# Fused chunked scan and two feed-forward layers: the order of halves, weight sums and wide rounds around a pair of token tiles

## The chip, the core and the metric

The kernel runs as one program on one core of a Trainium2 chip. The metric is device time in microseconds (us): the median of several executions, each the time of the whole program. A profile is one further execution, recorded by the hardware profiler. Engines are named as the profile names them: PE (TensorE matmul; PEld its weight load), DVE (VectorE), ACT (ScalarE), POOL (GpSimd), SP (SyncE, which here issues nearly all DMAs).

## The reference

Shapes: batch 4, 8 heads, 768 positions, head size 32, state size 16; so 3072 tokens of 256 features. All is float32.

```python
# per chunk c: cum = cumsum(log a), state carried from chunk to chunk
M = (Cc @ Bc^T) * exp(cum_i - cum_j) * (i >= j)
y = M @ xc + (Cc @ state) * exp(cum)
state = exp(sum log a) * state + sum_j Bc_j (x) xc_j * exp(cum_last - cum_j)
# tokens x 256, d_ff 768
x = maximum(maximum(x @ w1, x @ w2), x @ w3) @ w_out
# d_ff 2048
h = x @ w_in
out = (maximum(h, 0) + alpha * minimum(h, 0)) @ w_out2
```

## The kernel before

**Numbers.** Every float32 operand of a large product is kept as two parts, high (`gh`, index 0) and low (`gl`, index 1). A product of two blocks is three matmuls (`parts`, L658): high by high, low by high, high by low. `split` makes the parts: ACT copies the high part (L142), then POOL or, where the call says so, DVE subtracts it from the source (L143). The names in the traces are those of the tiles: `up` and `at` are PSUM tiles of products, `g` the result of a nonlinearity, `e` copies in SBUF.

**Attention.** The scan goes over 24 blocks of 128 tokens (`NR`). Each block is a round, cut into steps that a list `todo` holds; the two layers take steps from it between their products, at a rate that `quota` works out. The steps of a block are: `att_a` (POOL scales b and c), `att_s` (ACT and POOL make the parts of b and c in one tile, `tok`), `att_t` (DVE transposes `tok` and SP writes it to DRAM, `sc<-ts`, L394 to L400), `att_l` (SP reads it back in another order, `v<-sc` and `st<-sc`, L428 and L430), `att_e` (ACT exponentials, POOL mask), `att_b` (PE multiplies c by b, L473; DVE multiplies by the decay, L475), `att_u` (state; it also issues the broadcast load `e<-cum_w` of the next block), `att_y` (PE makes y, L541 and L544). From round 6 on the order is that of `fine`; the list entries of a round are: (1) a and half of e; (2) y, u and s; (3) b; (4) t; (5) l; (6) the loads of b, c and x and the other half of e.

**Layers.** Tiles of 512 tokens go through layer 1 (three up products per block of 128 features, a maximum, a down product) and layer 2 (one up product, a leaky rectifier, a down product). The last two tiles are the **pair**. For them `pair1` and `pair` use a scheme with seven block products in place of eight: blocks a11 to a22 of the weights, b11 to b22 of the tokens, sums s1 to s4 of the former and t1 to t4 of the latter. One such group is a **quad**, n = 0 to 7 in layer 1 (`QUADS1`), with f, j = divmod(n, 3); j is which of w1, w2, w3. A quad's PE order is a11, s2, s1, a12, s4, s3, (a11 of the next quad, in `begin`), a22. `keep` copies a PSUM tile to SBUF on ACT (L931); PE may only go on adding to that tile after it. DVE adds the kept tiles at L983 and L1019 (j > 0) or L986 (j = 0). After j = 2 a block of features is whole: `ready` splits it and puts its down product on the list `downs`, and `go_down` issues one (six matmuls); `POPS` says in which quads.

**Weight sums.** s1 to s4 come from `quad_sums(n)` in three steps: an addition of 128x512 (L812, POOL), four additions of 128x128 (L815 to L818, DVE), a split (ACT, POOL). The first three quads' sums are made by `prepare` during the last tile before the pair; in `pair1` quad n steps through `quad_sums(n + 2)`, all three steps within that quad:

```python
            more = quad_sums(n + 2) if n else None
...
            if j == 2:
                ready(tb, f, nc.vector)
                ready(ta, f)
                ready(ta, f2)
                held.append((tb, f2))
```

The third product of the last features is done plainly (`plain1`, four of them). `rows` and `columns` then make t1 to t4 for layer 2, and `pair` begins layer 2 with three plain up products, two down products and a fourth up product.

Of the kernel before, what the change touches and what calls it, by code (L numbers as in the profile page):

```python
# [15 lines left out]
ALU = mybir.AluOpType  # L16
# [9 lines left out]
NR = BT * NB  # L26
# [10 lines left out]
HALF = NF2 // 2  # L37
# [3 lines left out]
QUADS1 = 3 * HALF1 - 1  # L41
# [47 lines left out]
def fused(ctx: ExitStack, tc: tile.TileContext, x, a, B, C, w1, w2, w3, w_out, v_in, v_out, alpha, cst, out):  # L89
# [443 lines left out]
    def att_y(r):  # L533
# [41 lines left out]
            nc.vector.tensor_tensor(xt[t][1][:, g, o], yp[g], xt[t][0][:, g, o], ALU.subtract)  # L575
        del blk[r]

    def rounds(r0):

        for r in range(r0, NR):  # L580
            if r >= FINE:
                yield from fine(r)
                continue
            if r + 2 < NR:
                yield lambda r=r: att_a(r + 2), 0
            yield lambda r=r: (att_y(r), r + 1 < NR and att_u(r + 1)), r + 1
            if r + 2 < NR:
                late = r + 2 == NDIR
                yield lambda r=r, late=late: (att_e(r + 1), late or att_s(r + 2)), 0
                yield lambda r=r, late=late: (att_b(r + 1), att_s(r + 2) if late else att_t(r + 2)), 0  # L590
                yield lambda r=r, late=late: (late and att_t(r + 2), att_l(r + 2), load(r + 3)), 0
            elif r + 1 < NR:
                yield lambda r=r: att_e(r + 1), 0
                yield lambda r=r: att_b(r + 1), 0
# [208 lines left out]
    def corner(n):  # L803
        f, j = divmod(n, 3)
        if n < QUADS1:
            return [w[:, j].rearrange("p k (h f) -> p h k f", h=2)[:, :, :, f * P:(f + 1) * P] for w in w123]
        q = PLAIN + n - QUADS1
        return [w.rearrange("p k (h f) -> p h k f", h=2)[:, :, :, q * P:(q + 1) * P] for w in vi]

    def quad_sums(n):  # L810
        v, u = (v_tile().bitcast(F32).rearrange("p (i f) -> p i f", i=4) for _ in range(2))
        nc.gpsimd.tensor_tensor(v.rearrange("p (h k) f -> p h k f", h=2), *corner(n), ALU.add)  # L812
        yield
        a11, a12, a21, a22 = (v[:, i, :] for i in range(4))
        nc.vector.tensor_tensor(u[:, 0, :], a21, a22, ALU.add)  # L815
        nc.vector.tensor_tensor(u[:, 1, :], u[:, 0, :], a11, ALU.subtract)
        nc.vector.tensor_tensor(u[:, 3, :], a12, u[:, 1, :], ALU.subtract)
        nc.vector.tensor_tensor(u[:, 2, :], a11, a21, ALU.subtract)  # L818
        yield
        split(*[w[:, n % NSUM] for w in sums_0], u)  # L820
        yield
# [34 lines left out]
    def columns():  # L856
        p = acc[1, PAIR[1]]
        t1 = step(tall[0], p[0], ALU.subtract)
        t2 = step(tall[1], t1, ALU.subtract)

        def more():
            t4 = step(p[1], t2, ALU.subtract)
            split(*sum_b[0], t1, nc.vector)
            split(*sum_b[1], t2)
            later.append(lambda: split(*sum_b[3], t4))

        later.append(more)
# [3 lines left out]
    def prepare():  # L871
        nc.vector.tensor_scalar(rest, alph, -1.0, 1.0, ALU.mult, ALU.add)
        for n in range(NSUM):
            yield from quad_sums(n)
        while todo:
            yield
        yield from sums_of_x()
# [23 lines left out]
    def block(p, a, b, n, first):  # L901
        w, r = stationary(a, n), moving(b, n)
        parts(p, [w[0]], [w[1]], [r], first, True)
# [25 lines left out]
    def keep(p):  # L929
        e = em.tile([P, 512], F32, tag="e", name="e")  # L930
        nc.scalar.activation(e, p, AF.Copy)  # L931
        return e
# [10 lines left out]
    def pair1():  # L943
# [16 lines left out]
        def go_down():  # L960
            if carry:
                carry.pop(0)()
            elif downs:
                t, f, h = downs.pop(0)
                down((1, t), f, 0, 512, h)
                if f == NF1 - 1:
                    leave1((1, t))

        def ready(t, f, engine=nc.gpsimd):
            h_, l_ = place1()  # L970
            split(h_, l_, g[t, f], engine)
            downs.append((t, f, (h_, l_)))
# [21 lines left out]

        a, b = begin(0)
        later.pop()()
        for n in range(QUADS1):
            f, j = divmod(n, 3)
            f2 = HALF1 + f
            if carry:  # L1000
                go_down()
            more = quad_sums(n + 2) if n else None
            block(a, "s2", "t2", n, False)
            u2 = keep(a)
            c = ptile(ps_up, "up")
            block(c, "s1", "t1", n, True)
            p5 = keep(c)
            block(b, "a12", "b21", n, False)
            top(tb, f, j, b)
            more and next(more, None)  # L1010
            if carry or 0 in POPS.get(n, ()):
                go_down()
            block(c, "s4", "b22", n, False)
            both(c, u2, ta, f, j)
            while held:
                ready(*held.pop(0))
            block(a, "s3", "t3", n, False)
            if j:
                nc.vector.tensor_tensor(p5, a, p5, ALU.add)  # L1019
                top(ta, f, j, c)  # L1020
                top(ta, f2, j, p5)
            else:
                both(a, p5, ta, f2, j)
            if n + 1 < QUADS1:
                after = begin(n + 1)
            more and next(more, None)
            if 1 in POPS.get(n, ()):
                go_down()
            block(a, "a22", "t4", n, False)
            top(tb, f2, j, a)  # L1030
            more and next(more, None)
            if j == 2:
                ready(tb, f, nc.vector)
                ready(ta, f)
                ready(ta, f2)
                held.append((tb, f2))
            if n + 1 < QUADS1:
                a, b = after
        f, f2 = HALF1 - 1, NF1 - 1
        more = quad_sums(QUADS1 + 2)  # L1040

        def plain1(t, f):
            p = up_mm([w[:, 2, :, f * P:(f + 1) * P] for w in w123], xt[t], 0, 512)
            top(t, f, 2, p)
            ready(t, f, nc.vector if f == f2 else nc.gpsimd)

        for _ in range(3):
            next(more, None)
        for t, f, n in ((ta, f, 0), (ta, f2, 1), (tb, f, 1), (tb, f2, 1)):
            plain1(t, f)  # L1050
            for _ in range(n):
                go_down()
        rows()
        while downs:
            go_down()
        columns()

    def pair():
        ta, tb = PAIR
# [24 lines left out]
        def plain(t, f):  # L1084
            p = up_mm([w[:, :, f * P:(f + 1) * P] for w in vi], yt[t], 0, 512)
            return t, f, rectify(p, f)

        u = plain(ta, 0)
        u2 = plain(ta, HALF)
        ready(*u)  # L1090
        u = plain(tb, 0)
        ready(*u2)
        later.pop()()
        go_down()
        ready(*u)
        go_down()
        held = plain(tb, HALF)
        more = prepare_a(1)
        for q in range(PLAIN, HALF - 1):
            f, f2 = q, HALF + q  # L1100
# [205 lines left out]
```

## Time and profile before

| | us |
|---|---|
| median of 3 runs | 568.26 |
| lowest and highest | 565.99, 568.77 |
| the profiled execution, its own time | 564.66 |
| its span, first to last instruction | 562.9 |
| mean granted TensorE clock | 0.984 |

| engine | busy us | share of span |
|---|---|---|
| PE | 535.5 | 95% |
| DVE | 369.9 | 66% |
| ACT | 269.3 | 48% |
| POOL | 269.8 | 48% |

The granted clock is a share of full speed (1.0 is 2.4 GHz, 0.5 is 1.2 GHz); a busy PE at 0.5 does half the work. The attention ends at about 374 us of the span, layer 1 of the pair runs from about 393 to 471, layer 2 of the pair after it.

### The profile page before, as it was taken

How to read it: one execution, taken by the hardware profiler on the slowest of the kernel's cores; microseconds unless marked ns; L12 is line 12 of the kernel's file. 1: busy time of each engine (PE TensorE's matmuls, PEld its weight loads, DVE VectorE, ACT ScalarE, POOL GpSimd, SP SyncE). 2: the span in 40 equal slices, each digit the busy share in tenths (PEclk: the TensorE clock that was granted, in tenths of full speed). 3: DMA queues.
4: the chain of work that ended last, by engine and by line, in shares of the span. 5: the costliest groups of instructions: out<-in, count | busy, mean ns of one | idle time of the engine just before them, and what ended most of it. 6: DMA issues, size and time to landing. Idle time of an engine off the chain costs nothing.

```text
span 562.9 us, 9656 instructions
## 1 busy us (share of the span) xinstructions
PE 535.5 (95%) x3378; PEld 427.6 (76%) x3379; DVE 369.9 (66%) x657; ACT 269.3 (48%) x641; POOL 269.8 (48%) x287
## 2 busy tenths in 40 slices
PE   8889999999999989999999999989979878999997
PEld 4778888887888878878887887758757756778886
DVE  5886885989964357664456677768465655676453
ACT  6667775565444324443244234413443525666651
POOL 2143443335563326554236455747364651785651
PEclk9998999999999999999999999979989999999999
DMA  8877886786645665655744566400200000000024
GB/s 147 222 159 169 204 164 174 190 196 182 143 114 106 127 137 118 132 119 123 139 116 99 109 127 146 95 0 1 38 0 1 0 0 2 1 2 0 1 37 113
DMA packets 209344, 55.60 MB, mean 99 GB/s; under 512 B 159632, under 2 KB 201168, under 8 KB 209296
## 3 DMA queue, kind: packets, MB, share of 16 engines
q1 hardware_dynamic: 206928, 54.46, 43.8%
q10 hardware_dynamic: 2368, 0.52, 0.4%
q8 instruction: 27, 0.44, 0.4%
q14 instruction: 21, 0.17, 0.1%
HBM read 44.35 MB, written 10.62 MB: 98 GB/s over the span
## 4 chain that ended last, share of the span: by engine, by line
PE 64%; DVE 11%; ACT 7%; issue 7%; DMA 5%; POOL 3%; SPq 2%; ACTq 0%; DVEq 0%; POOLq 0%
PE up L658 31%; PE acc L658 21%; PE at L658 6%; DMA e<-cum_d 2%; POOL gl L143 1%; ACT gh L142 1%; DMA sc<-ts 1%; PE at L473 1%; PE at L544 1%; ACT e L456 1%; DVE v L184 1%; DVE g L684 1%; DMA b<-in_B_dram 1%; DMA xm<-in_x_dram 1%; SPq L400 1%
## 5 line engine op out<-in xcount | busy, mean ns | idle before, releaser
L143 POOL TENSOR_TENSOR gl<-g,gh 128x512 fp32r<-128x512 f32 (+1 forms) x102 | 128.8, 1263 | 174.1 <-ACT gh L142 165.6
L142 ACT ACTIVATE gh<-g 128x512 fp32r<-128x512 f32 (+1 forms) x107 | 64.7, 607 | 168.4 <-DVE g L697 104.7
L658 PE MATMUL up<-xt,w 128*128 128x512 f32 (+1 forms) x621 | 135.6, 362 | 0.7 <-ACT xt L574 0.6
L658 PEld LDWEIGHTS up<-xt,w 128*128 128x128 f32 x621 | 105.3, 193 | 20.6 <-issue 2.4
L658 PE MATMUL up<-yt,vi 128*128 128x512 f32 x459 | 117.7, 393 | 0.0
L658 PEld LDWEIGHTS up<-yt,vi 128*128 128x128 f32 x459 | 86.9, 190 | 18.4
L658 PE MATMUL acc<-gh,vo 128*128 128x512 f32 x268 | 84.9, 398 | 0.0
L696 DVE TENSOR_SCALAR g<-up,alph 128x512 f32<-128x512 f32 x64 | 47.7, 745 | 31.1 <-PE up L658 28.2
L684 DVE TENSOR_TENSOR g<-up,g 128x512 f32<-128x512 f32 (+1 forms) x60 | 34.7, 578 | 39.7 <-PE up L658 37.7
L658 PEld LDWEIGHTS acc<-gh,vo 128*128 128x128 f32 x268 | 49.6, 190 | 10.9 <-issue 0.6
L658 PE MATMUL acc<-gl,vo 128*128 128x512 f32 x134 | 53.0, 395 | 0.2
L697 DVE SCALAR_TENSOR_TENSOR g<-up,g 128x512 f32<-128x512 f32 x64 | 44.2, 691 | 2.2
L456 ACT ACTIVATE e<-e,ncum 128x128 f32<-128x128 f32 x120 | 38.0, 388 | 0.0
L658 PE MATMUL acc<-gh,wo 128*128 128x512 f32 (+1 forms) x136 | 37.4, 359 | 0.4 <-ACT gh L142 0.3
L143 POOL TENSOR_TENSOR sums<-v,sums 128x512 fp32r<-128x512 f32 x11 | 14.2, 1290 | 34.5 <-ACT sums L142 34.5
L658 PEld LDWEIGHTS acc<-gl,vo 128*128 128x128 f32 x134 | 25.5, 190 | 6.6 <-POOL gl L143 1.2
L658 PEld LDWEIGHTS acc<-gh,wo 128*128 128x128 f32 x136 | 23.8, 190 | 4.8 <-DVE yt L725 0.6
L184 DVE SCALAR_TENSOR_TENSOR v<-st,v 128x512 uint32<-128x512 uint32 x28 | 25.1, 896 | 2.8 <-ACT st L175 1.2
L658 PE MATMUL acc<-gl,wo 128*128 128x512 f32 (+1 forms) x68 | 24.0, 353 | 0.0
L457 POOL TENSOR_SCALAR_AFFINE_SELECT e<-e 128x512 f32<-128x512 f32 x30 | 19.9, 662 | 7.4 <-ACT e L456 7.4
L682 ACT ACTIVATE g<-up 128x512 f32<-128x512 f32 (+1 forms) x30 | 15.2, 505 | 13.3 <-PE up L658 11.4
L575 DVE TENSOR_TENSOR xt<-at,xt 128x128 fp32r<-128x128 f32 x48 | 11.9, 285 | 14.0 <-ACT xt L574 14.0
(241 smaller groups left out, 866.6 us busy)
## 6 DMA issues: line engine op xcount, KB each, us to landing
e<-cum_w SPq DMA_DIRECT2D x30, 256.0 KB, 4.5
st<-sc SPq DMA_DIRECT2D x60, 128.0 KB, 2.5
sc<-ts SPq DMA_DIRECT2D x52, 112.0 KB, 2.4
st<-in_moe_w_out_dram SPq DMA_DIRECT2D x11, 512.0 KB, 5.5
st<-in_moe_w_dram SPq DMA_DIRECT2D x9, 512.0 KB, 5.1
st<-in_moe_w_in_dram SPq DMA_DIRECT2D x8, 512.0 KB, 4.3
v<-sc SPq DMA_DIRECT2D x60, 64.0 KB, 2.1
out_dram<-st SPq DMA_DIRECT2D x20, 128.0 KB, 3.0
```

The costliest lines, as they stand in the source:

```text
L142: nc.scalar.activation(dst_h, src, AF.Copy)
L143: engine.tensor_tensor(dst_l, src, dst_h, ALU.subtract)
L184: nc.vector.scalar_tensor_tensor(v, hi, 3, v, ALU.logical_shift_left, ALU.bitwise_or)
L400: nc.sync.dma_start(sc[:used, :, o].rearrange("s (v q) t -> q (s v) t", v=4), ts[o, :used * P].rearrange("q (w t) -> q w t", t=32))
L456: nc.scalar.activation(e[:, q, :], e[:, q, :], AF.Exp, bias=ncum[:, k, b, 4 * g + q:4 * g + q + 1])
L457: nc.gpsimd.affine_select(out=e, in_=e, pattern=[[0, 4], [1, P]], compare_op=ALU.is_ge, fill=0.0, base=0, channel_multiplier=-1)
L575: nc.vector.tensor_tensor(xt[t][1][:, g, o], yp[g], xt[t][0][:, g, o], ALU.subtract)
L658: nc.tensor.matmul(acc, w, r, start=(first and i == 0), stop=(last and i == len(todo_) - 1), skip_group_check=True)
L682: nc.scalar.activation(g, p, AF.Copy)
L684: nc.vector.tensor_tensor(g, p, g, ALU.max)
L696: nc.vector.tensor_scalar(g, p, 0.0, alph[:, f:f + 1], ALU.min, ALU.mult)
L697: nc.vector.scalar_tensor_tensor(g, p, 0.0, g, ALU.max, ALU.add)
```

## The change

1. From round 10 on (`NDIR + 1`) the order of a round is `wide_round`: `att_s` goes to the front with `att_a`, `att_t` comes ahead of `att_y` and `att_u`, and `att_l` comes with `att_b`.
2. `quad_sums` takes the engine of its first addition: DVE in `prepare`, POOL in `pair1`.
3. In `pair1` the sums of quad n + 3 are begun at the end of quad n (the POOL addition) and go on in the next quad, after a12 (DVE) and after `begin` (the split).
4. Whole blocks of features are all put on `held` and split one by one in the next quad: after s1 (DVE), after a12 (POOL), after s4 (POOL), after a22 (DVE).
5. In the four plain products, the parts of the first tile's two blocks are made by DVE.
6. `columns` moves to `pair`, behind the first plain product of layer 2; the first product's low part is made by DVE, and four up products stand ahead of the first down product.

```diff
@@ attention
+    def wide_round(r):
+        more, near = r + 2 < NR, r + 1 < NR
+        if near:
+            yield lambda: (more and (att_a(r + 2), att_s(r + 2)), att_e(r + 1, 1)), 0
+        if more:
+            yield lambda: att_t(r + 2), 0
+        yield lambda: (att_y(r), near and att_u(r + 1)), r + 1
+        if near:
+            yield lambda: (att_b(r + 1), more and att_l(r + 2)), 0
+        if more:
+            yield lambda: load(r + 3), 0
+            yield lambda: att_e(r + 2, 0), 0
...
+            if r >= NDIR + 1:
+                yield from wide_round(r)
+                continue
@@ quad_sums, prepare
-    def quad_sums(n):
+    def quad_sums(n, engine=nc.gpsimd):
...
-        nc.gpsimd.tensor_tensor(v.rearrange("p (h k) f -> p h k f", h=2), *corner(n), ALU.add)
+        engine.tensor_tensor(v.rearrange("p (h k) f -> p h k f", h=2), *corner(n), ALU.add)
...
-            yield from quad_sums(n)
+            yield from quad_sums(n, nc.vector)
@@ pair1
-            more = quad_sums(n + 2) if n else None
             block(a, "s2", "t2", n, False)
             u2 = keep(a)
             c = ptile(ps_up, "up")
             block(c, "s1", "t1", n, True)
             p5 = keep(c)
+            if held:
+                ready(*held.pop(0), nc.vector)
             block(b, "a12", "b21", n, False)
             top(tb, f, j, b)
-            more and next(more, None)
+            go_on()
             if carry or 0 in POPS.get(n, ()):
                 go_down()
+            if held:
+                ready(*held.pop(0))
             block(c, "s4", "b22", n, False)
             both(c, u2, ta, f, j)
-            while held:
+            if held:
                 ready(*held.pop(0))
             block(a, "s3", "t3", n, False)
...
-            more and next(more, None)
+            go_on()
             if 1 in POPS.get(n, ()):
                 go_down()
             block(a, "a22", "t4", n, False)
             top(tb, f2, j, a)
-            more and next(more, None)
+            if held:
+                ready(*held.pop(0), nc.vector)
+            go_on()
             if j == 2:
-                ready(tb, f, nc.vector)
-                ready(ta, f)
-                ready(ta, f2)
-                held.append((tb, f2))
+                held.extend(((tb, f), (ta, f), (ta, f2), (tb, f2)))
+            more = quad_sums(n + NSUM)
+            next(more)
...
-            ready(t, f, nc.vector if f == f2 else nc.gpsimd)
+            ready(t, f, nc.vector if t == ta or f == f2 else nc.gpsimd)
...
-        columns()
@@ pair
         u = plain(ta, 0)
-        u2 = plain(ta, HALF)
+        columns()
+        ready(*u, nc.vector)
+        u = plain(ta, HALF)
         ready(*u)
         u = plain(tb, 0)
-        ready(*u2)
         later.pop()()
+        held = plain(tb, HALF)
         go_down()
         ready(*u)
         go_down()
-        held = plain(tb, HALF)
```

`go_on` takes the next step of `more`. After the change the lines of `parts` are L674, of `keep` L947, of L983, L986 and L1019 now L999, L1002 and L1044, and of the four small additions L831 to L834.

Three places in the order of instructions. The first is SP's queue in a wide round. Before, the load of the decay rows (`e<-cum_w`) stands ahead of the write of the transposed parts (`sc<-ts`):

```order
L238 DMA b<-in_B_dram 128x8x16
L238 DMA c<-in_C_dram 128x8x16
L248 DMA xm_108<-in_x_dram 128x8x32
L350 DMA e<-cum_w 128x4x128 x2
L400 DMA sc<-ts 32x28x32 x4
L423 DMA cpt<-sc 128x128
L428 DMA v<-sc 32x4x128
L430 DMA st<-sc 32x8x128
```

and in the changed kernel:

```order
L238 DMA b<-in_B_dram 128x8x16
L238 DMA c<-in_C_dram 128x8x16
L248 DMA xm_108<-in_x_dram 128x8x32
L400 DMA sc<-ts 32x28x32 x4
L350 DMA e<-cum_w 128x4x128 x2
L423 DMA cpt<-sc 128x128
L428 DMA v<-sc 32x4x128
L430 DMA st<-sc 32x8x128
```

The write moved ahead of the load; the eight reads `v<-sc`, `st<-sc` still follow.

The second is ACT between the third and the fourth quad of the pair's layer 1 (`up<-at` and `up<-up` are the copies in `begin`, `sums` the split of weight sums, `gh` and `st` high parts of whole blocks, `e` the copies of `keep`). Before:

```order
L992 ACTIVATE up<-at 128x512
L142 ACTIVATE sums_102<-v 128x512
L142 ACTIVATE gh<-g 128x512 x2
L142 ACTIVATE gh<-xm_108 128x512
L931 ACTIVATE e<-at 128x512
L931 ACTIVATE e<-up 128x512
L979 ACTIVATE xm_110<-up 128x512
L142 ACTIVATE st<-xm_109 128x512
```

and in the changed kernel:

```order
L1008 ACTIVATE up<-at 128x512
L142 ACTIVATE sums_102<-v 128x512
L947 ACTIVATE e<-at 128x512
L947 ACTIVATE e<-up 128x512
L142 ACTIVATE gh<-g 128x512
L995 ACTIVATE xm_110<-up 128x512
L142 ACTIVATE gh<-g 128x512
L142 ACTIVATE gh<-xm_108 128x512
```

The two copies of `keep` moved from behind three high parts to ahead of them.

The third is DVE in the second quad (n = 1) of the pair's layer 1. Before:

```order
L976 TENSOR_TENSOR g<-up,g 128x512
L983 TENSOR_TENSOR up<-up,e 128x512
L1019 TENSOR_TENSOR e<-at,e 128x512
L976 TENSOR_TENSOR g<-up,g 128x512
L976 TENSOR_TENSOR xm_108<-e,xm_108 128x512
L815 TENSOR_TENSOR v<-v 128x128
L816 TENSOR_TENSOR v<-v 128x128
L817 TENSOR_TENSOR v<-v 128x128
L818 TENSOR_TENSOR v<-v 128x128
```

and in the changed kernel:

```order
L992 TENSOR_TENSOR g<-up,g 128x512
L831 TENSOR_TENSOR v<-v 128x128
L832 TENSOR_TENSOR v<-v 128x128
L833 TENSOR_TENSOR v<-v 128x128
L834 TENSOR_TENSOR v<-v 128x128
L999 TENSOR_TENSOR up<-up,e 128x512
L1044 TENSOR_TENSOR e<-at,e 128x512
L992 TENSOR_TENSOR g<-up,g 128x512
L992 TENSOR_TENSOR xm_108<-e,xm_108 128x512
```

The four small additions moved ahead of the two that read the quad's product tiles.

## Rows read from the trace of the kernel before

**Rows 1.** The page, busy time of the engines over the span.

```profile
PE 535.5 (95%) x3378; PEld 427.6 (76%) x3379; DVE 369.9 (66%) x657; ACT 269.3 (48%) x641; POOL 269.8 (48%) x287
```

**Rows 2.** Waits of PE: who waited for whom, us in total, times, longest.

```profile
PE up L658 <- ACT e L931: 4.7, 3, 2.4
PE at L473 <- DMA b<-in_B_dram: 3.2, 2, 1.8
PE at L541 <- DVE e L475: 2.5, 1, 2.5
PE at L658 <- ACT gh L142: 1.8, 1, 1.8
PE at L658 <- POOL st L143: 1.8, 1, 1.8
PE at L658 <- ACT st L142: 1.3, 1, 1.3
...
PE at L658 <- POOL gl L143: 0.6, 1, 0.6
```

**Rows 3.** Stretches: length, PE, PEld, DVE, ACT, POOL busy, then granted clock.

```profile
198.00:202.00 4.00, 2.16 (x12) 1.57 (x11) 0.74 (x2) 0.60 (x1) 1.40 (x3) 1.00 0.70 147
371.31:378.05 6.74, 6.74 (x32) 4.89 (x33) 4.14 (x6) 1.58 (x5) 3.79 (x3) 0.52 0.00 0
418.50:422.30 3.80, 3.76 (x10) 2.97 (x10) 1.56 (x3) 0.99 (x2) 3.80 (x4) 0.55 0.00 0
463.00:467.00 4.00, 3.97 (x10) 3.13 (x11) 0.00 (x0) 0.11 (x1) 1.27 (x1) 0.57 0.02 4
```

**Rows 4.** Timeline, a round of attention: start, us, what, [idle before, releaser].

```profile
198.55 0.43 SPq L430 DMA_DIRECT2D st<-sc  x1
201.56 0.71 PE L473 MATMUL at<-st,v 128*128 128x256 f32 x4 [1.84 <-DMA b<-in_B_dram]
```

**Rows 5.** Timeline, the last round of attention, DVE and PE.

```profile
367.06 1.36 DVE L815 TENSOR_TENSOR v<-v 128x128 f32<-128x128 f32 x1 [1.75 <-POOL v L812]
371.31 0.69 PE L541 MATMUL at<-cpt,u 32*64 32x128 f32 x4 [2.53 <-DVE e L475]
```

**Rows 6.** Timeline, from the third to the fourth quad, ACT and PE.

```profile
415.33 0.63 ACT L142 ACTIVATE sums<-v 128x512 fp32r<-128x512 f32 x1 [1.76 <-DVE v L818]
415.87 1.13 ACT L142 ACTIVATE gh<-g 128x512 fp32r<-128x512 f32 x2
417.90 0.59 ACT L931 ACTIVATE e<-up 128x512 f32<-128x512 f32 x1
418.54 1.47 PE L658 MATMUL up<-xt,sums 128*128 128x512 f32 x3 [2.39 <-ACT e L931]
```

**Rows 7.** Timeline, the plain products of layer 1, DVE and PE.

```profile
458.07 0.29 DVE L815 TENSOR_TENSOR v<-v 128x128 f32<-128x128 f32 x1 [2.72 <-POOL v L812]
463.03 1.98 PE L658 MATMUL at<-st,wo 128*128 128x512 f32 x4 [1.76 <-POOL st L143]
```

**Rows 8.** Timeline, the start of layer 2, PE.

```profile
471.11 4.24 PE L658 MATMUL up<-yt,vi 128*128 128x512 f32 x18
477.14 0.73 PE L658 MATMUL at<-gh,vo 128*128 128x512 f32 x2 [1.79 <-ACT gh L142]
```

**Rows 9.** Timeline, the second quad, DVE and PE.

```profile
405.25 0.70 DVE L983 TENSOR_TENSOR up<-up,e 128x512 f32<-128x512 f32 x1 [0.32 <-PE up L658]
406.70 0.97 PE L658 MATMUL at<-yt,w 128*128 128x512 f32 x3 [0.15 <-DVE e L1019]
407.76 0.28 DVE L815 TENSOR_TENSOR v<-v 128x128 f32<-128x128 f32 x1
408.82 0.68 DVE L976 TENSOR_TENSOR xm<-at,xm 128x512 f32<-128x512 f32 x1
```

**Rows 10.** Timeline, two additions of SBUF tiles on DVE.

```profile
382.49 0.68 DVE L830 TENSOR_TENSOR e<-st 128x512 f32<-128x512 f32 x1
386.76 1.77 DVE L839 TENSOR_TENSOR e<-st 128x512 f32<-128x512 f32 x1
```

More of the change, by code (lines that the diff above doesn't have):

```diff
@@ L996, in pair1, with go_on @@
         later.pop()()
+        more = None
+        def go_on():
+            if more:
+                next(more, None)
         for n in range(QUADS1):
@@ L1039, in pair1 @@
         f, f2 = HALF1 - 1, NF1 - 1
-        more = quad_sums(QUADS1 + 2)
         def plain1(t, f):
@@ L1044, in plain1 @@
             top(t, f, 2, p)
-            ready(t, f, nc.vector if f == f2 else nc.gpsimd)
[L1047 to L1052, printed above, removed]
+            ready(t, f, nc.vector if t == ta or f == f2 else nc.gpsimd)
+        plain1(ta, f)
+        go_on()
+        plain1(ta, f2)
+        go_down()
+        plain1(tb, f)
+        go_on()
+        go_down()
+        plain1(tb, f2)
+        go_down()
         rows()
```

## The prediction

> **What bounds the kernel now.** The first view is the table of busy times: PE works 95% of the span and the next engine 66% [rows 1]. So PE sets the time, and a change that leaves PE's matmuls alone, as this one does, can win only two things: time in which PE stands still, and time in which its clock is low. The second view is the list of what PE waited for [rows 2]. The reader is to see that a few long waits make most of it, and that the waiting matmul and the releaser name the place: the attention's product with b and c (L473), the last round's y (L541), the copies of `keep` (ACT e L931), and halves of blocks that a down product needs (gh, gl, st). The third view, busy time by stretch, gives the clock [rows 3]: three stretches at a granted clock of 0.52 to 0.57, so nearly all at 1.2 GHz, and PE busy throughout. A stretch of length T at clock c holds T x c of full-speed work, so it loses T x (1 - c): 6.74 x 0.48 = 3.2, 3.80 x 0.45 = 1.7, 4.00 x 0.43 = 1.7 us. What went before is idle time of PE: each begins at or just before the end of a wait. Not every wait does this: 198 to 202 us holds a wait of 1.84 and stays at 1.00.
>
> The timeline then says why each wait is there.
>
> In attention, PE resumes at 201.56, 3.0 us after SP issued the last read `st<-sc` [rows 4]: SP is late, not b. The trace puts it down to the load of b.
>
> In the last round, DVE stands 1.75 us behind POOL's first addition of a weight sum (L812), and then needs 1.36 us for a small addition [rows 5]. Behind it stands the multiplication that frees the PSUM tile that y wants, so PE waits 2.53.
>
> Between the third and fourth quad, ACT waits 1.76 for DVE's part of a weight sum, then copies three high parts, and only then the tile of `keep`, at 417.90; PE waits 2.39 for it [rows 6]. The other two of the three such waits (4.7 in all, [rows 2]) have the same ACT order: a late split, or the same run of high parts after the sixth quad.
>
> In the plain products, DVE waits 2.72 us for another L812 while the first maximum stands behind it, so its halves come late and PE waits twice, 1.3 for the high and 1.76 for the low part [rows 2, 7]. At the start of layer 2, PE issues three products (18 matmuls in 4.24 us) and then waits 1.79 for the first block's high part, and 0.6 for its low part [rows 2, 8].
>
> **The change part by part.** No matmul is added or removed.
>
> *Wide rounds.* By the list, `att_l` comes six entries before its `att_b` instead of four, and `att_t` eight instead of five; a round has six. The two L473 waits are 1.8 and 1.4 us, 3.2 together [rows 2], and two entries are a third of a round, of which each holds several products. I take -3.2. SP meets the write ahead of the decay load, but that load waits for `att_y` to free its tile anyway. POOL gets one burst in place of two, and a transpose of DVE now comes one entry after the POOL work it reads; both lie beside PE, which has three up tiles to run ahead. New waits there could cost from nothing to the 3.2 that goes; below nothing they can't be, as no other wait of attention is long.
>
> *First sums on DVE.* The wait of 1.75 and the stretching (1.36 against 0.28 for the same addition elsewhere, [rows 5, 9], so 1.08) go, 2.8 in all, more than the 2.53 that PE waited. The added addition stands earlier in DVE's queue, where it has to share time with the layer's work: three of them, 0.68 to 1.77 each [rows 10]. That is covered by PE's lead; if the cover is gone, 0.5 to 1 us returns. With the wait goes the 3.2 of low clock behind it. I take -(2.5 + 3.2) + 0 = -5.7.
>
> *Halves one by one, sums earlier.* With the copies of `keep` ahead of the high parts, the 4.7 goes, and the 1.7 of low clock after the longest: -6.4. What is late next: (a) in quads with j > 0 the four small additions, 408.82 - 407.76 = 1.06 us, now stand ahead of L983 and L1019, and a22 already waits for L1019 [rows 9]. DVE was idle 0.32 before L983, so PE's wait grows by 1.06 - 0.32 = 0.7. In quads 4, 5 and 7 a down product stands between and covers it (six matmuls, at 4.24 / 18 each 1.4 us, [rows 8]); in quads 1 and 2 nothing does: +1.5. (b) In quads 3 and 6 a DVE split (0.68 to 1.77, as a SBUF addition, [rows 10]) and the four additions stand ahead of L986. From `keep` on PE has s4, s3, a11 and a down product, 3 x 0.7 + 1.4 = 3.5; DVE waits for the copy, 0.6 [rows 6], and has the split, 1.06 and two additions of 0.7 [rows 9], which is 3.7 to 4.8: 0.2 to 1.3 late. I take 0.3 each, near the short split, as POOL's halves queue behind this one: +0.6. In sum -4.3.
>
> *Plain products.* The POOL addition starts a quad earlier, so DVE doesn't wait, and the first tile's low parts come from DVE: -1.8 - 1.3, and -1.7 of low clock: -4.8. The cover of the chain maximum, copy, split (0.7 + 0.6 + 0.7) is the next plain product and the down product that `held` left over, 2.8 us.
>
> *Start of layer 2.* The fourth product gives PE 1.4 us of work, and two subtractions of 0.7 that stood ahead of the first rectifier on DVE now stand behind it: 2.8, against waits of 2.4. The second block's low part stays on POOL, and its rectifier stands behind DVE's split of the first. So between 0 and the 1.8 of before stays; I take 0.7, the short split: -1.7. `columns` later costs nothing while the two down products cover t1.
>
> Sum: -3.2 - 5.7 - 4.3 - 4.8 - 1.7 = **-19.7 us**. Against the profiled execution's 564.66 that is 545.0. The median of the runs is 568.26, 3.6 above it, and the change doesn't touch what differs between runs, so I forecast 568.26 - 19.7 = **548.5**.
>
> One row shows the same addition of two SBUF tiles at 0.68 and at 1.77 us [rows 10], and 1.36 for one that takes 0.28 [rows 5, 9]. The Trainium skill, "SBUF — State Buffer", section "Who interferes with whom", says that a DVE instruction with two SBUF inputs and a GpSimd instruction that reads SBUF lock each other out, the later one blocking fully. By that rule, work moved to DVE beside POOL's splits isn't cheap; the rows agree in kind, and the first rival prices it.
>
> **The rivals.** *DVE and POOL in each other's way.* In quads 1, 2, 3 and 6 the first small addition is stretched by 1.08, and in 3 and 6 the split by 1.09, all on PE's path: 4 x 1.08 + 2 x 1.09 = 6.5, and one fall of the clock at 1.7: 8.2 more, 556.7. For: the stretched rows. Against: POOL is busy 48% only [rows 1].
>
> *Half of it stays.* The loads of attention are late for another reason than their place (3.2 stays) and the clock falls at other waits (3.2 + 1.7 + 1.7): 9.8 more, 558.3. Against: the falls stand behind the waits that go.
>
> *The change only moves the wait.* Halves made one by one come after the down products that want them: seven down products in quads 3 to 7 and two behind, 2.1 each, would give all back, 567. Against: the first is wanted 2.1 us (three blocks) after `keep`, and copy and split take 1.3 to 2.4.
>
> *Slower.* From quad 1 on DVE reaches the small additions before POOL has made the first one, and L983, L1019 and a22 stand behind. The longest such wait seen is 2.72 [rows 7]; with a fall of 1.7 in each of seven quads this is 7 x 4.4 = 31 more, 579. It decides when the additions come over 1.5 us late per quad with the falls, or 3.2 without. Against: POOL has a whole a22 to s1 more than before.
>
> **How the numbers follow.** A measurement here tells about 0.5%, 2.8 us, from no change. Forecast 0.66 (its own range 544 to 552), first rival 0.17, second 0.09, third 0.04, slower 0.04. Faster is the first three, 0.92; same 0.04. The low end is all waits gone and no new ones (3.2 + 5.7 + 6.4 + 4.8 + 2.4 = 22.5) at the profiled execution's level, 542; the high end takes in both rivals that are still faster, 559.
>
> **What would show it.** In the waits of PE: no L473 for a load, no `keep` over 0.5, no L541 for DVE; new ones of about 0.8 for DVE e before a22 in quads 1 and 2. Clock 1.00 from 364 to 480 us. Layer 2's first product begins near 471.1 - 3.2 - 5.7 - 4.3 - 4.8 = 453 us. Wrong it would be if DVE waits for POOL in its small additions, if stretches at 0.5 are still there, or if the down products wait for halves.

## The result and the profile after

The changed kernel takes 560.44 us (median of 4 executions, 559.84 to 561.06), the kernel before in the same series 567.12 (564.09 to 568.77): ratio 0.9888, 95% interval [0.9841, 0.9936]. In a later series it took 559.65 us beside 567.53, ratio 0.9885 [0.9842, 0.9927]. The intervals lie below 1, so it is faster, by about 6.4 us or 1.1%, where 19.7 us (3.5%) were forecast; 560.44 stands above the 559 that the prediction named as its high end. (The ratio is an estimate from the single executions, not the quotient of the two medians.) The profiled execution took 561.06 us, span 559.2, mean granted clock 0.988.

The table of busy times is nearly that of [rows 1]:

```profile
PE 533.7 (95%) x3378; PEld 425.2 (76%) x3379; DVE 378.3 (68%) x664; ACT 270.9 (48%) x641; POOL 260.6 (47%) x280
```

What PE waited for, as in [rows 2] (us in total, times, longest):

```profile
PE at L473 <- DVE xt L575: 5.8, 3, 2.9
PE at L483 <- DVE xt L575: 2.4, 1, 2.4
PE at L674 <- DVE g L1002: 1.8, 1, 1.8
PE up L674 <- DVE g L1002: 1.8, 1, 1.8
...
PE up L674 <- DVE e L1044: 0.8, 2, 0.7
...
PE at L674 <- DVE e L1044: 0.7, 1, 0.7
PE at L674 <- POOL gl L143: 0.6, 1, 0.6
```

Every long wait at the head of [rows 2] is gone: the loads, the copies of `keep`, the last round's y, the halves in the plain products. In their place stand three waits of L473 for DVE's `xt` and two of 1.8 us for DVE's L1002. The clock, as in [rows 3]:

```profile
104.00:112.00 8.00, 6.19 (x22) 5.03 (x23) 5.79 (x12) 3.56 (x9) 2.17 (x3) 0.79 0.72 163
364.00:480.00 116.00, 108.84 (x495) 83.14 (x494) 83.79 (x137) 50.83 (x97) 58.71 (x45) 1.00 0.03 6
```

The three low stretches of before are at 1.00 in this execution, and a new one has come at 104 to 112 us (8 x 0.21 = 1.7 us lost).

To see where the time went, each profile is cut at three landmarks: ACT's first copy `yt<-acc` (the first tile leaves layer 1), PE's first product of the pair's layer 1, and PE's first product of layer 2 of the pair.

| profiled execution | start to first `yt` | A: to the pair | B: layer 1 of the pair | C: layer 2 of the pair to the end | span |
|---|---|---|---|---|---|
| before | 97.70 | 295.42 | 77.99 | 91.79 | 562.9 |
| after | 101.64 | 294.33 | 72.16 | 91.07 | 559.2 |
| forecast, difference | 0 | -8.9 | -9.1 | -1.7 | -19.7 |
| after, difference | +3.9 | -1.1 | -5.8 | -0.7 | -3.7 |

The +3.9 at the start is not the change's. It is L483's longer wait (2.35 at 76.65 us, 0.75 before) and a clock of 0.72 from 72 to 84 us, where PE still issues the same instructions in both kernels; the first that differs is the b-c product at 105.81. A second profile of the same kernel (below, `e5_after_again`) has 1.00 there, and its first `yt` at 97.43. It has two falls of the clock that the first profile has not, one in A and one in B, behind waits that both profiles have:

```profile
72.00:84.00 12.00, 10.90 (x183) 9.42 (x179) 8.91 (x23) 7.71 (x26) 6.53 (x10) 1.00 0.85 171
352.00:360.00 8.00, 6.97 (x25) 5.66 (x26) 7.01 (x13) 2.23 (x6) 3.80 (x3) 0.79 0.75 189
420.00:428.00 8.00, 6.16 (x21) 4.88 (x21) 3.92 (x9) 2.94 (x5) 2.95 (x3) 0.79 0.00 0
```

So A lacks nearly all of its 8.9 us (7.8 in the first profile, 8.7 in the second), B 3.3 or 4.8 of its 9.1, and C 1.0 of its 1.7.

**A, the b-c product at 105.81 us.** Two PSUM tiles of y are freed by DVE's L575, which stands behind ACT's copy L574; b takes such a tile. Timeline of the kernel before, its first y that is followed by a b of this kind:

```profile
96.58 0.65 PE L565 MATMUL at<-e,xm 128*32 128x64 f32 x32
97.27 1.66 PE L658 MATMUL up<-xt,w 128*128 128x512 f32 x6
...
100.56 2.90 PE L658 MATMUL up<-xt,w 128*128 128x512 f32 x12
101.23 0.42 ACT L574 ACTIVATE xt<-at 128x128 fp32r<-128x128 f32 x2
...
103.30 0.64 PE L473 MATMUL at<-st,v 128*128 128x256 f32 x4
```

and of the changed kernel:

```profile
100.52 0.65 PE L565 MATMUL at<-e,xm 128*32 128x64 f32 x32
101.22 1.66 PE L674 MATMUL up<-xt,w 128*128 128x512 f32 x6
...
104.64 0.63 ACT L188 ACTIVATE vi<-v 128x512 fp32r<-128x512 f32 x1 [1.46 <-DVE v L184]
105.17 0.43 ACT L574 ACTIVATE xt<-at 128x128 fp32r<-128x128 f32 x2
105.47 0.49 DVE L575 TENSOR_TENSOR xt<-at,xt 128x128 fp32r<-128x128 f32 x2 [0.26 <-ACT xt L574]
...
105.81 0.74 PE L473 MATMUL at<-st,v 128*128 128x256 f32 x4 [2.94 <-DVE xt L575]
```

L574 begins 4.65 us after y in both: 101.23 - 96.58 and 105.17 - 100.52. What changed is PE: before, an up product, a down product and two more up products stood between y and b; now the first of these alone does. Nothing in that round was written in another order, since it lies ahead of round 10. Its steps are only handed out faster: `quota` looks forward and divides the entries up to the next y's by the products left, and in a wide round y is the third entry where it was the second. Between y's last matmul and b's first stand 14 matmuls, where 32 stood. That `quota` is why b came up is read from the code; `e6_spacer`, below, tests the place of b itself.

**B, the fourth quad.** DVE, POOL and PE in the changed kernel (L831 to L834 are the four small additions, L1002 reads the quad's product tiles, the last line is a22):

```profile
420.70 0.28 DVE L831 TENSOR_TENSOR v<-v 128x128 f32<-128x128 f32 x1
...
421.14 1.33 POOL L143 TENSOR_TENSOR gl<-g,gh 128x512 fp32r<-128x512 f32 x1 [1.07 <-ACT gh L142]
421.35 1.27 DVE L833 TENSOR_TENSOR v<-v 128x128 f32<-128x128 f32 x1
...
422.42 1.33 POOL L143 TENSOR_TENSOR gl<-xm,gh 128x512 fp32r<-128x512 f32 x1
422.54 1.36 DVE L834 TENSOR_TENSOR v<-v 128x128 f32<-128x128 f32 x1
...
423.83 0.68 DVE L1002 TENSOR_TENSOR g<-up,e 128x512 f32<-128x512 f32 x1
...
425.16 0.96 PE L674 MATMUL at<-yt,w 128*128 128x512 f32 x3 [1.84 <-DVE g L1002]
```

L833 and L834 run beside POOL's two subtractions and take 1.27 and 1.36 us in place of 0.28, 2.1 more in all. L1002 stands behind them and a22 behind L1002. The seventh quad shows the same pair, 1.27 and 1.37, and a wait of 1.81.

**C, the start of layer 2** (PE and PEld in the changed kernel, as in [rows 8]):

```profile
468.13 6.25 PE L674 MATMUL up<-yt,vi 128*128 128x512 f32 x24
...
472.73 1.22 PEld L674 LDWEIGHTS up<-yt,vi 128*128 128x128 f32 x6 [0.47 <-DVE g L942]
...
477.47 0.50 PE L674 MATMUL at<-gl,vo 128*128 128x512 f32 x1 [0.63 <-POOL gl L143]
```

The 24 matmuls take 6.25 us, where 24 at the pace of [rows 8] would take 5.65: the fourth product has to wait for an up tile that DVE's rectifier has yet to read. And the second block's low part, still POOL's, is late by 0.63.

### The profile page after: what moved, and what is told of

Read it like the earlier page. It is cut to its first block, busy times and chain, and to the rows that moved or that the text cites. A ratio compares the mean times of both kernels' runs of the same rounds, so it can differ in the third digit from the quotient of the medians.

```text
span 559.2 us, 9630 instructions
## 1 busy us (share of the span) xinstructions
PE 533.7 (95%) x3378; PEld 425.2 (76%) x3379; DVE 378.3 (68%) x664; ACT 270.9 (48%) x641; POOL 260.6 (47%) x280
## 4 chain that ended last, share of the span: by engine, by line
PE 63%; DVE 15%; ACT 6%; issue 6%; DMA 5%; POOL 3%; SPq 1%; ACTq 0%; DVEq 0%; POOLq 0%
PE up L674 32%; PE acc L674 19%; PE at L674 7%; DMA st<-in_moe_w_in_dram 3%; DVE g L712 2%; ACT gh L142 2%; DVE v L184 1%; DVE g L713 1%; PE at L473 1%; DMA st<-in_moe_w_out_dram 1%; POOL gl L143 1%; PE at L544 1%; DMA e<-cum_d 1%; DVE ts L394 1%; DVE v L834 1%
## 5 line engine op out<-in xcount | busy, mean ns | idle before, releaser
L143 POOL TENSOR_TENSOR gl<-g,gh 128x512 fp32r<-128x512 f32 (+1 forms) x101 | 126.4, 1251 | 189.2 <-ACT gh L142 175.9
L674 PE MATMUL up<-xt,w 128*128 128x512 f32 (+1 forms) x621 | 135.4, 362 | 0.8 <-ACT xt L574 0.6
L674 PEld LDWEIGHTS up<-xt,w 128*128 128x128 f32 x621 | 105.0, 192 | 21.2 <-issue 2.4
L674 PE MATMUL up<-yt,vi 128*128 128x512 f32 x459 | 116.7, 390 | 0.1
L674 PEld LDWEIGHTS up<-yt,vi 128*128 128x128 f32 x459 | 85.9, 188 | 18.8 <-DVE g L942 0.5
L674 PE MATMUL acc<-gh,vo 128*128 128x512 f32 x268 | 83.9, 394 | 0.0
L674 PEld LDWEIGHTS acc<-gh,vo 128*128 128x128 f32 x268 | 49.0, 188 | 10.3 <-issue 0.4
L674 PE MATMUL acc<-gl,vo 128*128 128x512 f32 x134 | 52.6, 392 | 0.7 <-POOL gl L143 0.7
L674 PE MATMUL acc<-gh,wo 128*128 128x512 f32 (+1 forms) x136 | 38.0, 365 | 0.2 <-ACT gh L142 0.2
L674 PEld LDWEIGHTS acc<-gl,vo 128*128 128x128 f32 x134 | 25.2, 188 | 7.2 <-POOL gl L143 1.8
L674 PEld LDWEIGHTS acc<-gh,wo 128*128 128x128 f32 x136 | 24.4, 195 | 4.0 <-ACT gh L142 0.4
L674 PE MATMUL acc<-gl,wo 128*128 128x512 f32 (+1 forms) x68 | 24.8, 364 | 0.0
L175 ACT ACTIVATE st<-st 128x512 f32<-128x512 f32 x28 | 19.1, 681 | 4.6 <-DMA st<-in_moe_w_in_dram 2.9
```

The source lines that it names most:

```text
L143: engine.tensor_tensor(dst_l, src, dst_h, ALU.subtract)
L175: nc.scalar.activation(hi, hi, AF.Prelu, scale=2.0 ** -112, alpha=2.0 ** 32)
L674: nc.tensor.matmul(acc, w, r, start=(first and i == 0), stop=(last and i == len(todo_) - 1), skip_group_check=True)
```

## The experiments

Each series ran on one chip with the kernel before beside it (medians 564.36 us for e1 to e4, 567.53 for e5 to e8 and 565.0 for e9 to e12); across series ratios are compared. A and B are of one profiled execution each, so that one fall of the clock more or less, about 1.7 us, can lie between two of them. A tilde behind A: a wait of L473 for DVE's `xt` of 2 us or more lies in it.

| run | us | ratio to before, 95% | A | B |
|---|---|---|---|---|
| `e1_no_wide` | 557.38 | 0.9875 [0.9838, 0.9912] | 293.09 | 73.35 |
| `e2_wide_only` | 566.12 | 1.0015 [0.9987, 1.0042] | 296.19 ~ | 77.94 |
| `e3_quads` | 556.72 | 0.9857 [0.9825, 0.9889] | 295.45 ~ | 69.98 |
| `e4_gap` | 558.34 | 0.9887 [0.9848, 0.9925] | 293.56 ~ | 73.33 |
| `e5_after_again` | 559.65 | 0.9885 [0.9842, 0.9927] | 295.24 ~ | 73.73 |
| `e6_spacer` | 556.87 | 0.9839 [0.9796, 0.9881] | 292.11 ~ | 73.71 |
| `e7_no_wide_quads` | 553.13 | 0.9768 [0.9729, 0.9806] | 291.59 | 69.65 |
| `e8_gap_spacer_quads` | 551.11 | 0.9734 [0.9692, 0.9776] | 288.99 | 69.68 |
| `e9_all_quads` | 550.86 | 0.9738 [0.9711, 0.9764] | 288.94 | 70.20 |
| `e10_pool_sums` | 562.21 | 0.9942 [0.9912, 0.9971] | 297.20 ~ | 73.32 |
| `e11_repairs_pool_sums` | 553.83 | 0.9786 [0.9756, 0.9815] | 292.02 | 69.67 |
| `e12_repairs_again` | 549.83 | 0.9726 [0.9696, 0.9756] | 288.94 | 69.64 |

**The wide rounds, taken out and alone.** `e1_no_wide` is the changed kernel without these lines; `e2_wide_only` is the kernel before with them and `wide_round`:

```diff
-            if r >= NDIR + 1:
-                yield from wide_round(r)
-                continue
```

> The changed kernel with attention's rounds in their old order, all edits of the pair kept. Theory 1 (the wide rounds lost more than they won: 3.2 us of waits for a load went, 5.8 us of new waits of the b-c product for DVE's xt came, and 1.7 us of low clock at 104 to 112 us): this kernel is 4.3 us faster than the changed one's 560.4, so about 556; the product with b and c waits about 3.2 us for a load again, and for DVE xt under 1 us after 90 us of the span. Rival (those waits only take what PE would have stood still elsewhere, since the layer's work is as late): within 1.5 us of 560.4. On the stretch 72 to 84 us, ahead of the first instruction the change moves on PE: if it is of that one execution, the product L483 waits under 1 us and the clock is near 0.9 or more from 76 to 84; if the change causes it by a load, wait and low clock are gone here too, so this run alone can't tell, but a 2.35 us wait here would show it belongs to no wide round.

> The kernel before with the wide rounds alone. Theory 1: 3.2 us of waits for a load go, 5.8 us less the 2.0 at 357 us (which needed the first sums on DVE) come, with 1.7 us of low clock: 567.1 - 3.2 + 3.8 + 1.7 = 569.4, so not faster, 567 to 571. Rival (the prediction's term holds, and what is new comes from the pair's edits): 567.1 - 3.2 = 563.9.

Without the wide rounds the waits for a load are back (4.0 us, one of 2.48 and one of 1.53), those for `xt` are 0.2 in all. Against the changed kernel's 0.9885 the ratio of 0.9875 tells nothing: the intervals lie over each other. Alone, the wide rounds bring no gain, 1.0015, and A is 0.8 us longer. There the L473 waits for `xt` are 6.0 us, with low clock behind two of them, and both the waits for a load and the 2.53 of the last round's y are gone. That last was not expected: in A the terms for the wide rounds and for the first sums seem to reach for the same wait. L483 waited 1.5 in e1 and 2.0 in e2, and the clock from 72 to 84 us is 1.00 in both: the fall there belongs to single executions (of all the profiles only `e10_pool_sums` has one there too, behind a wait of 1.62).

**The small additions behind what reads the product tiles.** `e3_quads`:

```diff
             top(tb, f, j, b)
-            go_on()
+            if j or not n:
+                go_on()
...
                 both(a, p5, ta, f2, j)
+                if n:
+                    go_on()
```

> The changed kernel; in the fourth and seventh quad the four small additions of weight sums stand behind the two additions that read the quad's product tiles (not ahead). Theory 2 (DVE's small additions, stretched to 1.3 us each beside POOL's low parts, hold back those two): the waits of a22 for DVE g of 1.84 and 1.81 us fall under 0.5 each, 560.4 - 3.2 = 557. Rival (the split of a half on DVE and the copy of the product tile are what is late, the additions only fill the time): the waits stay over 1.3 each and the time within 1 us of 560.4. If the weight sums then come late for the quad three further on, new waits for sums stand in quads 6 and 7.

Both waits of a22 for L1002 are gone; B falls to 69.98. The interval of the ratio still lies over that of the changed kernel, so the reading rests on the trace. DVE in the fourth quad:

```profile
418.70 0.69 DVE L1002 TENSOR_TENSOR g<-up,e 128x512 f32<-128x512 f32 x1
420.28 0.69 DVE L1002 TENSOR_TENSOR g<-at,e 128x512 f32<-128x512 f32 x1 [0.89 <-POOL gl L143]
420.89 0.76 DVE L831 TENSOR_TENSOR v<-v 128x128 f32<-128x128 f32 x1
```

Shown: the additions were late, not the split (0.69) or the copy. The second L1002 waits 0.89 for POOL's low part, and a22 has no wait left all the same. New waits for DVE e L1045 (1.1 and 0.4, at a22 of the fifth and eighth quad) took 1.6 of the 3.65 us back.

**b further behind y.** `e4_gap` parts b from y in the wide rounds by putting l between:

```diff
         yield lambda: (att_y(r), near and att_u(r + 1)), r + 1
+        if more:
+            yield lambda: att_l(r + 2), 0
         if near:
-            yield lambda: (att_b(r + 1), more and att_l(r + 2)), 0
+            yield lambda: att_b(r + 1), 0
         if more:
-            yield lambda: load(r + 3), 0
-            yield lambda: att_e(r + 2, 0), 0
+            yield lambda: (load(r + 3), att_e(r + 2, 0)), 0
```

> The changed kernel with another order in a wide round: a, s and half of e; t; y and u; l; b; load and the other half of e. So the reading back comes one entry earlier and b two products' worth later behind y. Theory 1 (b stands too close behind y, whose tile DVE has not yet freed): the waits of the product with b and c for DVE xt fall from 5.8 to under 2, no waits for a load come back, 560.4 - 4 - 1.7 = 554.7. Rival (DVE's transposes ahead of y hold the tile, whatever stands between y and b): these waits stay over 4 and the time within 1.5 us of 560.4.

Half a hit. The waits at about 153 and 357 us are gone and L473 waits for no load, but 2.94 us at 103.28 us stay, with the low clock behind them, since rounds 8 and 9 are not wide. And y of the last round now waits 1.04 for DVE, b's products being later there. The ratio, 0.9887, is that of the changed kernel: alone, this edit gains no time that can be seen. `e6_spacer` treats rounds 8 and 9 alone, with an empty entry behind y in their old order:

```diff
+        if r >= NDIR - 1:
+            yield lambda: None, 0
         if near:
             yield lambda: (att_b(r + 1), r + 2 < NDIR and att_t(r + 2)), 0
```

> The changed kernel once more, as it is, as a base for the others of this series. If the wait of L483 and the low clock at 72 to 84 us belong to one execution, they are smaller here (wait under 2.0, clock 0.9 or more), and the first copy of yt (end of tile 0 in layer 1) comes at 97.5 to 99.5 us as in the other profiles, not at 101.6; its time is then about 558 to 559. If they belong to the changed kernel, 560 to 561 as before.

> The changed kernel with an empty entry between y and b in rounds 8 and 9 of attention, which still have the old order but are handed out faster, since the wide rounds behind them count one entry more up to each y. Theory 1 (b comes one entry too early behind y there): the wait of the product with b and c for DVE xt at about 105 us (2.9) goes, with the low clock at 104 to 112 us (1.7): 4 us faster than the changed kernel of this series; the waits at about 153 and 357 us (0.9 and 2.0) stay. Rival (DVE and ACT are late there because the weights are still being converted, wherever b stands): a wait of over 2 us stays, at this or the next product, and the time within 1 us.

`e5_after_again` has the waits of the first profile to a tenth (2.94, 2.03, 1.84, 1.81) and the shorter start. In `e6_spacer` the 2.94 is gone, 32 matmuls stand between y and b again, b comes at 104.29 without a wait, and the clock is whole there:

```profile
104.29 0.64 PE L473 MATMUL at<-st,v 128*128 128x256 f32 x4
```

```profile
102.00:114.00 12.00, 12.00 (x56) 10.00 (x55) 11.39 (x21) 6.43 (x15) 3.52 (x4) 1.00 0.81 209
```

A falls from 295.24 to 292.11, 3.1 us, for a step that does nothing; the medians of the two runs differ by 2.8, with intervals that still overlap. Shown: the wait came from where b was handed out, not from DVE or ACT. The waits at about 153 and 357 us stay, as foreseen.

**Two and three repairs together.** `e7_no_wide_quads` joins e1 and e3; `e8_gap_spacer_quads` joins e3, e4 and e6.

> Rounds in their old order and, in the fourth and seventh quad, the small additions behind the two that read product tiles: the two single edits together. If their gains are of different places they add: no waits of a22 for DVE g, and waits of b and c for a load of 3 to 4 us, time 1.5 to 2.5 us under the run without wide rounds, 2 us under the run with the quads' edit alone at equal disturbance: about 554.5 beside 564.4 of before. Rival (without waits at 105 us the clock falls elsewhere): as the quads' edit alone, 556.7.

> All three repairs: b one entry behind y in wide rounds with l ahead of it, an empty entry in rounds 8 and 9, small additions behind in the fourth and seventh quad. Theory 1 and 2: the waits of L473 fall under 1 us in all, those of a22 in the two quads under 0.5, no load is waited for: 5.8 - 1 + 1.7 + 3.2 = 9.7 under the changed kernel's 558 to 560, so 549 to 551. Rival (PE's idle time moves on to y of the last round, where 1.0 us appeared with this order, and to low parts): 553 to 555.

e7 came out at 0.9768, and against e3's 0.9857 the intervals are apart: with the fourth and seventh quad mended, the wide rounds as written cost 0.9%, some 5 us. How much they cost is not fixed by that: e1 against the changed kernel showed 0.1%, and by A they cost 1.2 to 2.2 us there and 3.9 here (295.45 against 291.59). e8, with the wide rounds mended, is at 0.9734, which can't be told from e7's 0.9768; its A is 2.6 us below e7's, in one profile each. So the idea of the wide rounds is worth something near the 3.2 us that the prediction gave it, once b is not pulled up behind y, but only A says so.

**Every quad.** `e9_all_quads` moves `go_on` behind the L1044 and L1002 additions in all quads:

```diff
             top(tb, f, j, b)
-            if j or not n:
-                go_on()
...
-                if n:
-                    go_on()
+            go_on()
```

> As the run with all three repairs, but in every quad the small additions stand behind the additions that read product tiles, not only in the fourth and seventh. Theory (the 0.7 us waits of a22 for DVE e in the second and third quad are these four additions, 1.06 us ahead of them less 0.3 of idle time): both waits go, 1.4 us faster than the run with three repairs. Rival (the copy of the kept tile is as late, or the weight sums now come late): the waits stay over 0.4, or waits for sums appear, and the time is the same within 1 us or longer.

> The run with three repairs once more, as the base of this series: 551 beside 564 to 567 of the kernel before; waits of L473 under 0.5 in all, no low clock but at 44 us.

The rival held: the two waits of 0.7 go (0.15 is left), and two of 0.84 come, at s4 of the next quad, for the copy of `keep` (`L950`), with 0.60 more for a low part. A row of the first of them:

```profile
405.43 0.96 PE L677 MATMUL up<-xt,sums 128*128 128x512 f32 x3 [0.84 <-ACT e L950]
```

Behind the small additions ACT splits the sums, ahead of `keep`; later additions make that split late. 550.86 us and 549.83 of e12 can't be told apart. e12 repeats e8, and its clock is 1.00 through the pair:

```profile
350.00:480.00 130.00, 124.10 (x559) 94.51 (x558) 95.62 (x159) 59.77 (x114) 71.98 (x53) 1.00 0.07 16
```

**The first sums back on POOL**, in the changed kernel and in that with three repairs:

```diff
-            yield from quad_sums(n, nc.vector)
+            yield from quad_sums(n)
```

> The changed kernel, with the first additions of the first three weight sums on POOL as before. Theory 3 (wide rounds alone already take away the wait of y in the last round, so the prediction counted it a second time for the sums on DVE): no wait of L541 over 0.5, waits for DVE xt at 105, 153 and 357 us as in the changed kernel, time within 1.5 us of its 559.65. Rival (the sums on DVE are what takes that wait away): a wait of y of about 2.5 us with low clock behind it, 4 to 5.7 us slower, 563.5 to 565.

> The run with three repairs, with the first additions of the first three weight sums on POOL. Theory 3: within 1.5 us of the run with three repairs. Rival: L541 waits 2.5 and the clock falls, 4 to 5.7 us slower. Since with three repairs b stands later behind y than in the changed kernel, DVE's wait for POOL's sum can stand ahead of the last decay product here though not there; then L541's 1.0 us of that run grows by about 1.4 and the time by 1.4 to 4.

Theory 3, formed on e2, fell. In e10 y waits 1.49, the clock is 0.79 from 376 to 384 us behind it, and A is 2.0 to 2.9 us longer than in the two profiles of the changed kernel; in e11 the old picture is back, DVE behind POOL's addition:

```profile
365.16 1.30 POOL L831 TENSOR_TENSOR v<-w,w 128x512 f32<-128x512 f32 x1
...
366.49 1.36 DVE L834 TENSOR_TENSOR v<-v 128x128 f32<-128x128 f32 x1 [1.75 <-POOL v L831]
...
370.75 0.43 PE L541 MATMUL at<-cpt,u 32*64 32x128 f32 x4 [2.53 <-DVE e L475]
```

A is 292.02 against 288.94, so here the first sums on DVE are worth 3.1 us: 1.5 of the wait (2.53 against e12's 1.03) and 1.7 of low clock (0.57 from 372 to 376). That the wide rounds alone also lose this wait holds for e2 and not for e10: DVE waits 0.21 us for POOL's third addition in e2 (before its L831 at 370.75) and 1.70 in e10 (at 374.02). What makes that addition late in the one and not in the other was not followed up.

e1 and e7 test the same term without wide rounds: there the first sums on DVE are the only edit in A. The wait of L541 falls from 2.53 to under 0.2, and A from 295.42 to 293.09 and 291.59, 2.3 and 3.8 us.

## Why the prediction was wrong

The direction was right, the size a third. Of the signs that it named, those on the waits and the clock came: no L473 for a load, no `keep` over 0.5, no L541, about 0.7 before a22 in two quads (0.8 was named), 1.00 from 364 to 480 us in the first profile, though not in the second (0.79 from 420 to 428). The one on time did not: layer 2's first product stands at 468.13, not at 453. And one sign of being wrong came, in a place that the prediction did not watch: low clock, at 104 to 112 us. By its own terms:

**Wide rounds, -3.2: this step failed.** The waits for a load went as forecast. But the step said new waits "could cost from nothing to the 3.2 that goes" and took nothing, since PE has "three up tiles to run ahead". What ran out was no up tile but one of `at`, which y and b share. The new waits cost 5.84 us (2.94, 0.87, 2.03) and 1.7 of low clock (3.4 in the second profile), so by the waits the term came out near +4.3. It looked at how many entries lie between the steps that moved, not at what the new place of y in the list does to the pace of the steps ahead of it. The largest new wait arose in a round that the edit doesn't touch. e6 shows this cause by itself, e4 the closeness of b and y in the wide rounds.

**First sums on DVE, -5.7: right, too large.** In the changed kernel both the wait and the fall behind it are gone. What that is worth was measured at 2.3 and 3.8 us without wide rounds (e1 and e7) and at 3.1 with the repairs (e11 and e12). The clock's part was half of what [rows 3] had, 1.7 in e11, and waits of 0.5 for a low part came instead. The three large additions (0.69 to 1.55 us on DVE) were covered, as forecast. With the repairs 1.0 of L541 is left: in e12 the four small additions ahead of that y's decay product take 2.5 us (0.41, 0.60, 1.27 and 0.28) where they took 1.06 in [rows 9]. That these leave the 1.0 is likely, but no run tests it.

**Halves one by one, -4.3: right but for (b).** The waits for `keep` went. (a) came near: a22 in the second and third quad waits 0.67 and 0.69, where 0.7 more than the 0.15 of before was worked out. (b) said 0.3 each for the fourth and seventh quad, "near the short split"; they wait 1.84 and 1.81. The split was short (0.69); the small additions, counted at 1.06 for the four, took 3.2, two of them beside POOL's low parts. The rows for that were at hand: [rows 5] has one at 1.36. By its waits the term of -4.3 came out near -1.7. This is the first rival's mechanism, in two of the four quads that it named. Its price of 8.2 was too high: nothing was stretched in the second and third quad, and no low clock lay there in this execution (in the second profile one fall did, behind the 1.84). The Trainium skill, "SBUF — State Buffer", section "Who interferes with whom", has a GpSimd instruction that reads SBUF and a DVE instruction with two SBUF inputs shut each other out: the runs agree, 0.28 us alone against 1.27 to 1.37 beside POOL, and each ends 0.15 us behind one of POOL's subtractions (421.35 + 1.27 = 422.62 and 421.14 + 1.33 = 422.47; 423.90 and 423.75). L832, which began at 421.02, ahead of that subtraction's 421.14, took 0.29.

**Plain products, -4.8: right.** None of its waits is left, and the clock is whole; no run takes this part out by itself. With the quads mended B is 69.64, 8.35 below before, of 9.1 forecast for B in all.

**Start of layer 2, -1.7: 0.7.** The low part's 0.63 stayed, as the 0.7 that was kept back. What the step missed is that the fourth product has no free tile: 0.6 of the 1.4 us that it was to give PE passes in a wait.

**The base.** 19.7 off 568.26 was also a high start: this median of three stands above the later ones of 11 to 17 executions, 564.36 to 567.53.

In sum, of the 13.3 us between forecast and result, by stages, 8 to 9 lie in A, 3 to 5 in B, depending on which of the two profiles one takes, and 1.0 in C. The repairs of e8 and e12 give 9 of them back: 0.9726 to 0.9734, so about 15 us below before. Of the 4 to 5 us still missing 1.0 is in C, and the waits of 1.0 (L541) and 1.6 (a22 of the fifth and eighth quad) stand in no term of the forecast; the rest is open.

The rivals: "half of it stays" was nearest with 558.3, but not for its reason, since no load was late. "Only moves the wait" is wrong for the halves, and right in another place, b behind y. The slower case did not happen: none of the small additions in the pair's layer 1 waits for POOL.

## What to carry to other kernels

Where a list of steps is handed out by a rate, an entry put ahead of a deadline speeds up every step before it; look in the new instruction order at how many products stand between a matmul that frees or takes a PSUM tile and the one that wants it, in the untouched rounds too. When small DVE instructions are moved ahead of the one that PE needs, price each of them at its longest row beside POOL, not at its shortest. And whether two edits claim the same wait is seen only by taking each out of the whole as well as putting it in alone: by themselves the wide rounds removed y's wait (e2), in the changed kernel they did not (e10).

## What the hardware showed beyond that

How the clock answers a wait was not the same from one execution to the next. Over the profile of before, the first of the changed kernel and the twelve of the experiments: behind the wait of 2.9 us at the first b the clock fell in 6 of 6; behind y's 2.53 in 2 of 2; behind the 2.0 to 2.25 at about 355 us in 4 of 6; behind the 1.8 of a22 in the fourth and seventh quad in 5 of 12; and behind the 2.48 for a load in e1 not at all. Most falls cost about 1.7 us (4 us at 0.57, or 8 us at 0.79), the one behind y in the kernel before 3.2 [rows 3]. The other two falls that the prediction counted came in both profiles that have their waits (`keep`'s 2.39 and the plain products' 1.76, before and e2). But the mean granted clock of the kernel before ran from 0.975 to 0.996 over its executions: at 0.996 some 2.2 us of 560 are lost, less than the 6.6 of the three counted falls together. So gains that the prediction took as sure were partly chance. The Trainium skill, "TensorE: Matmul & The Clock Gate", section "What's actually happening", says that the monitor behind the gate runs free and isn't set back when a kernel starts; executions that differ with equal waits agree with that, though no run here shows the monitor itself.
